# Full 128 x 128 tiles for every matmul of a pooling-attention and MLP-mixer kernel: padding in place of 64-row and 64-column operands

## The chip, the core and the metric

One core of a Trainium2 chip runs the whole kernel. The time is the device time of one launch in microseconds (us), from the first instruction to the last. The kernel before takes 377.35 us, the median of 4 runs (375.98 to 378.72).

## What is computed

Two networks one after the other, for 8 batch elements of 576 positions. First an attention of 8 heads of 64, whose keys and values are averaged over groups of 8 positions, so that there are 72 of each. Then a mixer: an MLP over the positions (256 wide) and an MLP over the channels (1536 wide), each added to its input.

```python
# q, k, v: (8, 8, 576, 64) float32
k_p = k.reshape(B, H, 72, 8, D).mean(axis=3)
v_p = v.reshape(B, H, 72, 8, D).mean(axis=3)
scores = 1/sqrt(D) * (q @ k_p.transpose(0, 1, 3, 2))
attn = softmax(scores)
x = (attn @ v_p) -> (B, 576, 512)
u = x + (relu(x^T @ w_tok1) @ w_tok2)^T       # w_tok1 576 x 256, w_tok2 256 x 576
out = u + relu(u @ w_ch1) @ w_ch2             # w_ch1 512 x 1536, w_ch2 1536 x 512
```

## The kernel before

All matmuls are bf16 with sums in float32. 576 positions are four chunks of 128 and a tail of 64; `csize = [128, 128, 128, 128, 64]`. TensorE (PE) multiplies a stationary operand `lhsT`, loaded into the array by a weight load (PEld), with a moving operand `rhs`; the profile gives the two as rows of `lhsT` * columns of `lhsT`, so 128*64 is an `lhsT` of 128 rows and 64 columns. Three stages stand for one batch element each. Stage A is the attention:

```python
# pool k (pool v, s_pool_v, is the same into its own bank, after all of k)
            for c in range(NC):
                cs = csize[c]
                nc.tensor.matmul(out=kp_ps, lhsT=p_full[0:cs, c, :], rhs=kb[0:cs, c].rearrange("p h d -> p (h d)"),
                                 start=(c == 0), stop=(c == NC - 1))
            nc.vector.tensor_copy(out=kp_sb, in_=kp_ps)
# transpose the pooled k, head by head: 64 columns each, to partitions 0..63 or 64..127
            for h in range(H):
                pr, hl = h // 2, h % 2
                nc.tensor.transpose(out=kpT_ps[hl * D:(hl + 1) * D, pr, 0:SP], in_=kp_sb[:, h, :],
                                    identity=ident[0:SP, 0:SP])
            nc.vector.tensor_copy(out=kpT_sb, in_=kpT_ps[:, :, 0:SP])
# transpose q
                qT_ps = ps_tr.tile([P, H // 2, P], BF16, name="pt")
                for pr in range(H // 2):
                    nc.tensor.transpose(out=qT_ps[:, pr, 0:cs],
                                        in_=qb[0:cs, c, 2 * pr:2 * pr + 2, :].rearrange("p h d -> p (h d)"),
                                        identity=ident[0:cs, 0:cs])
                nc.scalar.copy(out=qT_sb[:, :, c * P:c * P + cs], in_=qT_ps[:, :, 0:cs])
# scores of one head: 64 rows of lhsT
            def s_score():
                pr, hl = h // 2, h % 2
                sc_ps = ps_big.tile([SP, 512], FP32, name="pa")
                sc_ps2 = ps_small.tile([SP, S - 512], FP32, name="pb")
                nc.tensor.matmul(out=sc_ps, lhsT=kpT_sb[hl * D:(hl + 1) * D, pr, :],
                                 rhs=qT_sb[hl * D:(hl + 1) * D, pr, 0:512], start=True, stop=True)
                nc.tensor.matmul(out=sc_ps2, lhsT=kpT_sb[hl * D:(hl + 1) * D, pr, :],
                                 rhs=qT_sb[hl * D:(hl + 1) * D, pr, 512:S], start=True, stop=True)
                nc.scalar.activation(out=expT_sb[:, h, 0:512], in_=sc_ps, func=AF.Exp, scale=scale)
                nc.scalar.activation(out=expT_sb[:, h, 512:S], in_=sc_ps2, func=AF.Exp, scale=scale)
# attention times v, for one chunk and four heads; the 65th column is the sum of exp
                cs = csize[c]
                ao_ps = ps_small.tile([P, 4, D + 1], FP32, name="pb")
                for hh in range(4):
                    h = half * 4 + hh
                    nc.tensor.matmul(out=ao_ps[0:cs, hh, :], lhsT=expT_sb[:, h, c * P:c * P + cs],
                                     rhs=vp_sb[:, h, :], start=True, stop=True)
                den_r = out_pool.tile([P, 4], FP32, name="den")
                nc.vector.reciprocal(out=den_r[0:cs], in_=ao_ps[0:cs, :, D])
                bcast = den_r[0:cs, :, None].broadcast_to([cs, 4, D])
                nc.vector.tensor_tensor(out=x_sb[0:cs, c, half * 4 * D:(half + 1) * 4 * D].rearrange("p (h d) -> p h d", d=D),
                                        in0=ao_ps[0:cs, :, 0:D], in1=bcast, op=ALU.mult)
# ...
        steps += [mk_av(c, half) for c in range(NC) for half in range(2)]
```

Stage B is the MLP over the positions, stage C the one over the channels:

```python
# stage B
                at_ps = ps_big.tile([P, DM], FP32, name="pa")
                for c in range(NC):
                    cs = csize[c]
                    nc.tensor.matmul(out=at_ps, lhsT=w_tok1_sb[0:cs, c, m * P:(m + 1) * P], rhs=x_sb[0:cs, c, :],
                                     start=(c == 0), stop=(c == NC - 1))
# ...
                u_ps = ps_big.tile([P, DM], FP32, name="pa")
                for m in range(2):
                    nc.tensor.matmul(out=u_ps[0:cs, :], lhsT=w_tok2_sb[:, m, c * P:c * P + cs], rhs=AT_sb[:, m, :],
                                     start=(m == 0), stop=(m == 1))
                nc.vector.tensor_tensor(out=u_sb[0:cs, c, :], in0=u_ps[0:cs, :], in1=x_sb[0:cs, c, :], op=ALU.add)
                uT_ps = ps_tr.tile([P, 4, P], BF16, name="pt")
                for kk in range(4):
                    nc.tensor.transpose(out=uT_ps[:, kk, 0:cs], in_=u_sb[0:cs, c, kk * P:(kk + 1) * P],
                                        identity=ident[0:cs, 0:cs])
# ... copied to uT by ScalarE (c even) or VectorE (c odd)
# stage C
                g_ps = ps_big.tile([P, 512], FP32, name="pa")
                g_ps2 = ps_small.tile([P, S - 512], FP32, name="pb")
                for kk in range(4):
                    nc.tensor.matmul(out=g_ps, lhsT=w_ch1_sb[:, kk, m * P:(m + 1) * P], rhs=uT_sb[:, kk, 0:512],
                                     start=(kk == 0), stop=(kk == 3))
                for kk in range(4):
                    nc.tensor.matmul(out=g_ps2, lhsT=w_ch1_sb[:, kk, m * P:(m + 1) * P], rhs=uT_sb[:, kk, 512:S],
                                     start=(kk == 0), stop=(kk == 3))
# ... relu to GT on ScalarE (m even) or VectorE (m odd)
            def s_out():
                cs = csize[c]
                o_ps = ps_big.tile([P, DM], FP32, name="pa")
                for kk in range(12):
                    nc.tensor.matmul(out=o_ps[0:cs, :], lhsT=GT_sb[:, kk, c * P:c * P + cs], rhs=w_ch2_sb[:, kk, :],
                                     start=(kk == 0), stop=(kk == 11))
                o_sb = out_pool.tile([P, DM], FP32, name="o")
                nc.vector.tensor_tensor(out=o_sb[0:cs, :], in0=o_ps[0:cs, :], in1=u_sb[0:cs, c, :], op=ALU.add)
                nc.scalar.dma_start(out=out[b, c * P:c * P + cs, :], in_=o_sb[0:cs, :])
```

PSUM, in which matmuls put their sums, is handed out from three pools: `ps_big` (tiles "pa", 4 buffers), `ps_small` (tiles "pb", 2 buffers) and `ps_tr` (tiles "pt" of transposes, 2 buffers). The stages are a software pipeline: in turn `it` the kernel runs A of element `it`, B of element `it - 1` and C of element `it - 2`, their steps woven into one another. So there are 10 turns, of which turns 2 to 7 hold all three stages. The loads of `q`, `k` and `v` for the next element are DMAs that GpSimd issues at the start of a turn; the four weight matrices are loaded at the start of the kernel.

Of the kernel before, what the change touches and what calls it, by code (L numbers as in the profile page):

```python
# [8 lines left out]
FP32 = mybir.dt.float32  # L9
# [6 lines left out]
def kernel(  # L16
# [48 lines left out]
    w_tok2_sb = singles.tile([P, 2, S], BF16)  # L65
# [3 lines left out]
    with tc.tile_pool(name="wtmp", bufs=1) as wtmp:  # L69
# [9 lines left out]
        nc.vector.tensor_copy(out=w_tok2_sb, in_=wf2)  # L79
# [22 lines left out]

    def stage_A(qb, kb, vb, x_sb):
        kp_sb = att_pool.tile([SP, H, D], BF16, name="kp")
        vp_sb = att_pool.tile([SP, H, D + 1], BF16, name="vp")
        kpT_sb = att_pool.tile([P, H // 2, SP], BF16, name="kpT")
        qT_sb = att_pool.tile([P, H // 2, S], BF16, name="qT")
        expT_sb = att_pool.tile([SP, H, S], BF16, name="expT")
        steps = []

        def s_pool_k():
            kp_ps = ps_big.tile([SP, H, D], FP32, name="pa")
            for c in range(NC):
                cs = csize[c]
                nc.tensor.matmul(out=kp_ps, lhsT=p_full[0:cs, c, :], rhs=kb[0:cs, c].rearrange("p h d -> p (h d)"),  # L115
                                 start=(c == 0), stop=(c == NC - 1))
            nc.vector.tensor_copy(out=kp_sb, in_=kp_ps)
        def s_pool_v():
            vp_ps = ps_big.tile([SP, H, D], FP32, name="pa")
            for c in range(NC):  # L120
                cs = csize[c]
                nc.tensor.matmul(out=vp_ps, lhsT=p_full[0:cs, c, :], rhs=vb[0:cs, c].rearrange("p h d -> p (h d)"),  # L122
                                 start=(c == 0), stop=(c == NC - 1))
            nc.gpsimd.memset(vp_sb[:, :, D], 1.0)  # L124
            nc.vector.tensor_copy(out=vp_sb[:, :, 0:D], in_=vp_ps)
        def s_kpT():
            kpT_ps = ps_tr.tile([P, H // 2, P], BF16, name="pt")
            for h in range(H):
                pr, hl = h // 2, h % 2
                nc.tensor.transpose(out=kpT_ps[hl * D:(hl + 1) * D, pr, 0:SP], in_=kp_sb[:, h, :],  # L130
                                    identity=ident[0:SP, 0:SP])
            nc.vector.tensor_copy(out=kpT_sb, in_=kpT_ps[:, :, 0:SP])
        steps += [s_pool_k, s_pool_v, s_kpT]

        def mk_qT(c):
            def s_qT():
                cs = csize[c]
                qT_ps = ps_tr.tile([P, H // 2, P], BF16, name="pt")
                for pr in range(H // 2):
                    nc.tensor.transpose(out=qT_ps[:, pr, 0:cs],  # L140
                                        in_=qb[0:cs, c, 2 * pr:2 * pr + 2, :].rearrange("p h d -> p (h d)"),
                                        identity=ident[0:cs, 0:cs])
# [4 lines left out]
        def mk_score(h):  # L147
            def s_score():
# [3 lines left out]
                nc.tensor.matmul(out=sc_ps, lhsT=kpT_sb[hl * D:(hl + 1) * D, pr, :],  # L152
                                 rhs=qT_sb[hl * D:(hl + 1) * D, pr, 0:512], start=True, stop=True)
                nc.tensor.matmul(out=sc_ps2, lhsT=kpT_sb[hl * D:(hl + 1) * D, pr, :],  # L154
                                 rhs=qT_sb[hl * D:(hl + 1) * D, pr, 512:S], start=True, stop=True)
# [5 lines left out]
        def mk_av(c, half):  # L161
            def s_av():
                cs = csize[c]
                ao_ps = ps_small.tile([P, 4, D + 1], FP32, name="pb")
                for hh in range(4):
                    h = half * 4 + hh
                    nc.tensor.matmul(out=ao_ps[0:cs, hh, :], lhsT=expT_sb[:, h, c * P:c * P + cs],  # L167
                                     rhs=vp_sb[:, h, :], start=True, stop=True)
                den_r = out_pool.tile([P, 4], FP32, name="den")
                nc.vector.reciprocal(out=den_r[0:cs], in_=ao_ps[0:cs, :, D])  # L170
                bcast = den_r[0:cs, :, None].broadcast_to([cs, 4, D])
                nc.vector.tensor_tensor(out=x_sb[0:cs, c, half * 4 * D:(half + 1) * 4 * D].rearrange("p (h d) -> p h d", d=D),  # L172
                                        in0=ao_ps[0:cs, :, 0:D], in1=bcast, op=ALU.mult)
            return s_av
        steps += [mk_av(c, half) for c in range(NC) for half in range(2)]
        return steps

    def stage_B(x_sb, u_sb, uT_sb):
        AT_sb = moe_pool.tile([P, 2, DM], BF16, name="AT")
        steps = []  # L180
        def mk_AT(m):
            def s_AT():
                at_ps = ps_big.tile([P, DM], FP32, name="pa")
                for c in range(NC):
                    cs = csize[c]
                    nc.tensor.matmul(out=at_ps, lhsT=w_tok1_sb[0:cs, c, m * P:(m + 1) * P], rhs=x_sb[0:cs, c, :],  # L186
# [8 lines left out]
        def mk_u(c):  # L195
            def s_u():
                cs = csize[c]
                u_ps = ps_big.tile([P, DM], FP32, name="pa")
                for m in range(2):
                    nc.tensor.matmul(out=u_ps[0:cs, :], lhsT=w_tok2_sb[:, m, c * P:c * P + cs], rhs=AT_sb[:, m, :],  # L200
# [14 lines left out]
    def stage_C(b, u_sb, uT_sb):  # L215
        GT_sb = moe_pool.tile([P, 12, S], BF16, name="GT")
# [51 lines left out]
    for it in range(B + 2):  # L268
# [5 lines left out]
        if ba < B:  # L274
# [5 lines left out]
            x_sb = x_pool.tile([P, NC, DM], BF16, name="x")  # L280
            xbuf[ba] = x_sb
            A_steps = stage_A(qb, kb, vb, x_sb)
# [43 lines left out]
```

The softmax here doesn't subtract the row's maximum and nothing guards it: scores larger than these inputs give would overflow.

## Time and profile before

| what | value |
|---|---|
| time, median of 4 runs | 377.35 us |
| span of the profiled run | 377.0 us |
| TensorE matmul busy | 329.2 us, 87% of the span, 2280 recorded |
| TensorE weight load busy | 161.1 us, 43% |
| VectorE busy | 160.8 us, 43% |
| ScalarE busy | 117.7 us, 31% |
| GpSimd busy | 106.3 us, 28% |
| DMA | 31.44 MB, mean 83 GB/s |

Engines: PE is a TensorE matmul, PEld a TensorE weight load, which runs beside matmuls; DVE is VectorE, ACT ScalarE, POOL GpSimd. "L223" is line 223 of the kernel. The end of a matmul in the profile is modelled and matmuls overlap in the array, so the duration of one says little; the distance from one start to the next is what one costs in a stream. A few per cent of the matmul records are missing from the trace.

### The profile page before, as it was taken

Reading aid. Unit: us, or ns where it says so; the run is one execution under the profiler, and the core shown is the slowest. Engines: PE = TensorE matmul, PEld = TensorE weight load, DVE = VectorE, ACT = ScalarE, POOL = GpSimd, SP = SyncE. Lnnn points to the kernel's source line nnn. Section 1 sums busy time; section 2 is a strip of 40 time slices with the busy share of each in tenths; the row PEclk is TensorE's granted clock in tenths of the full one; section 3 lists DMA queues with packets and bytes.
Section 4 is the critical chain, followed back from the end, with each engine's and each line's share of the span. In section 5 each row is a group of like instructions: output and inputs, shape, how many; then the busy total and the mean of one; then the engine's idle time right before and its main releaser. Section 6 shows DMA issues by size and latency. Waiting matters only on the chain.

```text
span 377.0 us, 5649 instructions
## 1 busy us (share of the span) xinstructions
PE 329.2 (87%) x2280; PEld 161.1 (43%) x2320; DVE 160.8 (43%) x389; ACT 117.7 (31%) x299; POOL 106.3 (28%) x138
## 2 busy tenths in 40 slices
PE   0305459899999999999999999999999999999994
PEld 0003125355454544444545454445445454544542
DVE  1003026382655345634553365445552654443421
ACT  1005406527501660056104720364017501310300
POOL 9819369946103900193008400000000000000000
PEclk9999999999999999999999999999999999999999
DMA  9999999979823971299029902000210011002012
GB/s 137 235 291 123 314 166 117 147 51 104 54 76 66 129 46 57 70 124 66 30 84 106 98 13 99 16 2 0 86 42 2 1 71 57 0 28 92 7 57 70
DMA packets 120746, 31.44 MB, mean 83 GB/s; under 512 B 113232, under 2 KB 113808, under 8 KB 120720
## 3 DMA queue, kind: packets, MB, share of 16 engines
q0 software_dynamic: 112512, 14.16, 63.8%
q10 hardware_dynamic: 5248, 9.44, 7.2%
q1 hardware_dynamic: 2960, 7.47, 5.8%
q8 instruction: 18, 0.29, 0.3%
q14 instruction: 8, 0.07, 0.1%
HBM read 35.78 MB, written 9.44 MB: 120 GB/s over the span
## 4 chain that ended last, share of the span: by engine, by line
PE 82%; DMA 8%; POOL 5%; ACT 2%; issue 1%; DVE 1%; POOLq 0%
PE pa L242 27%; PE pa L223 23%; DMA kb<-in_k_dram 8%; PE pa L186 5%; PE pa L200 5%; PE pb L167 4%; PE pa L152 3%; PE pb L226 3%; PE pt L205 3%; PE pa L122 3%; PE pt L140 2%; PE pa L115 2%; POOL qb L99 2%; POOL vb L99 2%; POOL kb L99 1%
## 5 line engine op out<-in xcount | busy, mean ns | idle before, releaser
L242 PE MATMUL pa<-w_ch_sb,GT 128*128 128x512 bf16 (+1 forms) x472 | 111.9, 379 | 0.4
L223 PE MATMUL pa<-uT,w_ch_sb 128*128 128x512 bf16 x363 | 95.7, 380 | 2.0 <-issue 1.3
L242 PEld LDWEIGHTS <-GT 128*128 128x128 bf16 (+1 forms) x480 | 45.1, 100 | 45.3 <-issue 0.8
L245 DVE TENSOR_TENSOR o<-pa,u 128x512 f32<-128x512 f32 (+1 forms) x40 | 27.6, 690 | 58.2 <-PE pa L242 56.2
L232 DVE TENSOR_SCALAR GT<-pa 128x512 bf16<-128x512 f32 x48 | 33.1, 691 | 36.8 <-PE pa L223 36.6
L223 PEld LDWEIGHTS <-w_ch_sb 128*128 128x128 bf16 x384 | 31.7, 98 | 31.8 <-issue 7.7
L229 ACT ACTIVATE GT<-pa 128x512 bf16<-128x512 f32 x48 | 28.7, 597 | 52.6 <-PE pa L223 50.8
L208 ACT COPY uT<-pt 128x512 bf16<-128x512 bf16 (+1 forms) x24 | 12.3, 514 | 103.2 <-PE pt L205 103.2
L156 ACT ACTIVATE expT<-pa 72x512 bf16<-72x512 f32 x64 | 37.9, 599 | 18.6 <-PE pb L154 18.3
L115 PE MATMUL pa<-kb,p_full 128*72 128x512 bf16 (+1 forms) x40 | 14.4, 441 | 30.3 <-DMA kb<-in_k_dram 30.3
L99 POOL DMA_DIRECT2D vb<-in_v_dram x40 | 36.3, 915 | 13.8 <-DMA qb<-in_q_dram 11.9
L202 DVE TENSOR_TENSOR u<-pa,x 128x512 bf16<-128x512 f32 (+1 forms) x40 | 27.1, 677 | 30.4 <-PE pa L200 28.1
L143 ACT COPY qT<-pt 128x512 bf16<-128x512 bf16 (+1 forms) x40 | 21.1, 551 | 59.7 <-PE pt L140 59.1
L99 POOL DMA_DIRECT2D qb<-in_q_dram x40 | 35.3, 891 | 10.5 <-PE pt L140 5.8
L99 POOL DMA_DIRECT2D kb<-in_k_dram x40 | 35.1, 881 | 10.6 <-PE pt L205 9.4
L172 DVE TENSOR_TENSOR x<-pb,den 128x256 bf16<-128x256 f32 (+1 forms) x80 | 32.8, 417 | 1.3
L226 PEld LDWEIGHTS <-w_ch_sb 128*128 128x128 bf16 x384 | 23.4, 98 | 18.1 <-issue 0.2
L124 POOL MEMSET vp<- 72x8 bf16 x8 | 1.5, 186 | 94.8 <-issue 94.8
L167 PEld LDWEIGHTS <-expT 72*128 72x128 bf16 (+1 forms) x320 | 19.5, 106 | 17.9 <-issue 5.4
L226 PE MATMUL pb<-uT,w_ch_sb 128*128 128x64 bf16 x384 | 26.5, 193 | 0.1
L200 PE MATMUL pa<-AT,w_tok_sb 128*128 128x512 bf16 (+1 forms) x71 | 25.0, 408 | 1.2 <-ACT AT L189 0.8
L186 PE MATMUL pa<-x,w_tok_sb 128*128 128x512 bf16 (+1 forms) x78 | 24.3, 410 | 0.1
(44 smaller groups left out, 258.1 us busy)
## 6 DMA issues: line engine op xcount, KB each, us to landing
out_dram<-o ACTq DMA_DIRECT2D x32, 256.0 KB, 2.0
wf<-in_moe_w_ch_dram SPq DMA_DIRECT2D x2, 3072.0 KB, 13.8
qb<-in_q_dram POOLq DMA_DIRECT2D x32, 128.0 KB, 4.6
kb<-in_k_dram POOLq DMA_DIRECT2D x32, 128.0 KB, 4.7
vb<-in_v_dram POOLq DMA_DIRECT2D x32, 128.0 KB, 5.0
out_dram<-o ACTq DMA_DIRECT2D x8, 128.0 KB, 2.3
wf<-in_moe_w_tok_dram SPq DMA_DIRECT2D x1, 576.0 KB, 5.8
wf<-in_moe_w_tok_dram SPq DMA_DIRECT2D x1, 512.0 KB, 3.8
```

The costliest lines, as they stand in the source:

```text
L99: nc.gpsimd.dma_start(out=dst[0:cs, c], in_=src_[b, :, c * P:c * P + cs, :].rearrange("h p d -> p h d"))
L156: nc.scalar.activation(out=expT_sb[:, h, 0:512], in_=sc_ps, func=AF.Exp, scale=scale)
L167: nc.tensor.matmul(out=ao_ps[0:cs, hh, :], lhsT=expT_sb[:, h, c * P:c * P + cs], rhs=vp_sb[:, h, :], start=True, stop=True)
L172: nc.vector.tensor_tensor(out=x_sb[0:cs, c, half * 4 * D:(half + 1) * 4 * D].rearrange("p (h d) -> p h d", d=D), in0=ao_ps[0:cs, :, 0:D], ...
L186: nc.tensor.matmul(out=at_ps, lhsT=w_tok1_sb[0:cs, c, m * P:(m + 1) * P], rhs=x_sb[0:cs, c, :], start=(c == 0), stop=(c == NC - 1))
L200: nc.tensor.matmul(out=u_ps[0:cs, :], lhsT=w_tok2_sb[:, m, c * P:c * P + cs], rhs=AT_sb[:, m, :], start=(m == 0), stop=(m == 1))
L223: nc.tensor.matmul(out=g_ps, lhsT=w_ch1_sb[:, kk, m * P:(m + 1) * P], rhs=uT_sb[:, kk, 0:512], start=(kk == 0), stop=(kk == 3))
L226: nc.tensor.matmul(out=g_ps2, lhsT=w_ch1_sb[:, kk, m * P:(m + 1) * P], rhs=uT_sb[:, kk, 512:S], start=(kk == 0), stop=(kk == 3))
L229: nc.scalar.activation(out=GT_sb[:, m, 0:512], in_=g_ps, func=AF.Relu)
L232: nc.vector.tensor_scalar(out=GT_sb[:, m, 0:512], in0=g_ps, scalar1=0.0, scalar2=None, op0=ALU.max)
L242: nc.tensor.matmul(out=o_ps[0:cs, :], lhsT=GT_sb[:, kk, c * P:c * P + cs], rhs=w_ch2_sb[:, kk, :], start=(kk == 0), stop=(kk == 11))
L245: nc.vector.tensor_tensor(out=o_sb[0:cs, :], in0=o_ps[0:cs, :], in1=u_sb[0:cs, c, :], op=ALU.add)
```

## The change

Every matmul and every weight load gets more than 64 rows and more than 64 columns, by padding:

- The tail chunk of 64 positions is treated as 128. The tiles of `q`, `k`, `v`, `x`, `u` (rows) and of the exponentials, `GT` and `w_tok2` (columns) are made 640 positions long; what lies behind position 576 is set to zero once, at the start, and is never written again. So these tiles are no longer handed out by rotating pools: there are two of each, made once, and taken in turns.
- The scores of a head contract over 64 channels. The stationary operand becomes 128 rows, of which the 64 that belong to the other head of the pair are zero; the moving operand becomes both heads' q. The zeros are set once, and the copy of the transposed pooled k fills the other half.
- The pooled k is transposed in pairs of heads (4 transposes of 128 columns in place of 8 of 64), and copied out in 2 pieces in place of one.
- The pooling of k and that of v alternate chunk by chunk, in two banks, in place of all of k and then all of v.
- Attention times v handles both halves of the heads of a chunk in one step, alternating between the two "pb" buffers.

What is written to memory is the same 576 positions.

```diff
-    w_tok2_sb = singles.tile([P, 2, S], BF16)
+    w_tok2_sb = singles.tile([P, 2, NC * P], BF16)
 ...
+    kpT_z = [singles.tile([P, H, SP], BF16, name=f"kpTz{i}") for i in range(2)]
+    for t in kpT_z:
+        nc.vector.memset(t, 0.0)
+    SPAD = NC * P
+
+    def two(name, shape):
+        ts = [singles.tile(shape, BF16, name=f"{name}{i}") for i in range(2)]
+        for t in ts:
+            nc.vector.memset(t[TAIL:P, NC - 1], 0.0)
+        return ts
+    q_z, k_z, v_z = (two(n, [P, NC, H, D]) for n in ("qz", "kz", "vz"))
+    e_z = [singles.tile([SP, H, SPAD], BF16, name=f"ez{i}") for i in range(2)]
+    g_z = [singles.tile([P, 12, SPAD], BF16, name=f"gz{i}") for i in range(2)]
+    for t in e_z + g_z:
+        nc.vector.memset(t[:, :, S:SPAD], 0.0)
+    nc.vector.memset(w_tok2_sb[:, :, S:SPAD], 0.0)
+    x_z, u_z = (two(n, [P, NC, DM]) for n in ("xz", "uz"))
+
     def load_qkv(b):
-        qb = qkv_pool.tile([P, NC, H, D], BF16, name="qb")
-        kb = qkv_pool.tile([P, NC, H, D], BF16, name="kb")
-        vb = qkv_pool.tile([P, NC, H, D], BF16, name="vb")
+        qb, kb, vb = q_z[b % 2], k_z[b % 2], v_z[b % 2]
 ...
+    def stage_A(b, qb, kb, vb, x_sb):
 ...
-        kpT_sb = att_pool.tile([P, H // 2, SP], BF16, name="kpT")
+        kpT_sb = kpT_z[b % 2]
         qT_sb = att_pool.tile([P, H // 2, S], BF16, name="qT")
-        expT_sb = att_pool.tile([SP, H, S], BF16, name="expT")
+        expT_sb = e_z[b % 2]
 ...
         def s_pool_k():
             kp_ps = ps_big.tile([SP, H, D], FP32, name="pa")
+            vp_ps = ps_big.tile([SP, H, D], FP32, name="pa")
+            stage_A.vp_ps = vp_ps
             for c in range(NC):
                 cs = csize[c]
-                nc.tensor.matmul(out=kp_ps, lhsT=p_full[0:cs, c, :], rhs=kb[0:cs, c].rearrange("p h d -> p (h d)"),
+                nc.tensor.matmul(out=kp_ps, lhsT=p_full[:, c, :], rhs=kb[:, c].rearrange("p h d -> p (h d)"),
+                                 start=(c == 0), stop=(c == NC - 1))
+                nc.tensor.matmul(out=vp_ps, lhsT=p_full[:, c, :], rhs=vb[:, c].rearrange("p h d -> p (h d)"),
                                  start=(c == 0), stop=(c == NC - 1))
             nc.vector.tensor_copy(out=kp_sb, in_=kp_ps)
         def s_pool_v():
-            vp_ps = ps_big.tile([SP, H, D], FP32, name="pa")
-            for c in range(NC):
-                cs = csize[c]
-                nc.tensor.matmul(out=vp_ps, lhsT=p_full[0:cs, c, :], rhs=vb[0:cs, c].rearrange("p h d -> p (h d)"),
-                                 start=(c == 0), stop=(c == NC - 1))
+            vp_ps = stage_A.vp_ps
             nc.gpsimd.memset(vp_sb[:, :, D], 1.0)
             nc.vector.tensor_copy(out=vp_sb[:, :, 0:D], in_=vp_ps)
         def s_kpT():
             kpT_ps = ps_tr.tile([P, H // 2, P], BF16, name="pt")
-            for h in range(H):
-                pr, hl = h // 2, h % 2
-                nc.tensor.transpose(out=kpT_ps[hl * D:(hl + 1) * D, pr, 0:SP], in_=kp_sb[:, h, :],
+            for pr in range(H // 2):
+                nc.tensor.transpose(out=kpT_ps[:, pr, 0:SP],
+                                    in_=kp_sb[:, 2 * pr:2 * pr + 2, :].rearrange("p h d -> p (h d)"),
                                     identity=ident[0:SP, 0:SP])
-            nc.vector.tensor_copy(out=kpT_sb, in_=kpT_ps[:, :, 0:SP])
+            for hl in range(2):
+                nc.vector.tensor_copy(out=kpT_sb[hl * D:(hl + 1) * D, hl:H:2, :],
+                                      in_=kpT_ps[hl * D:(hl + 1) * D, :, 0:SP])
 ...
-                    nc.tensor.transpose(out=qT_ps[:, pr, 0:cs],
-                                        in_=qb[0:cs, c, 2 * pr:2 * pr + 2, :].rearrange("p h d -> p (h d)"),
-                                        identity=ident[0:cs, 0:cs])
+                    nc.tensor.transpose(out=qT_ps[:, pr, :],
+                                        in_=qb[:, c, 2 * pr:2 * pr + 2, :].rearrange("p h d -> p (h d)"),
+                                        identity=ident)
 ...
-                nc.tensor.matmul(out=sc_ps, lhsT=kpT_sb[hl * D:(hl + 1) * D, pr, :],
-                                 rhs=qT_sb[hl * D:(hl + 1) * D, pr, 0:512], start=True, stop=True)
-                nc.tensor.matmul(out=sc_ps2, lhsT=kpT_sb[hl * D:(hl + 1) * D, pr, :],
-                                 rhs=qT_sb[hl * D:(hl + 1) * D, pr, 512:S], start=True, stop=True)
+                nc.tensor.matmul(out=sc_ps, lhsT=kpT_sb[:, h, :],
+                                 rhs=qT_sb[:, pr, 0:512], start=True, stop=True)
+                nc.tensor.matmul(out=sc_ps2, lhsT=kpT_sb[:, h, :],
+                                 rhs=qT_sb[:, pr, 512:S], start=True, stop=True)
 ...
-        def mk_av(c, half):
+        def mk_av(c):
             def s_av():
                 cs = csize[c]
-                ao_ps = ps_small.tile([P, 4, D + 1], FP32, name="pb")
+                ao = [ps_small.tile([P, 4, D + 1], FP32, name="pb") for _ in range(2)]
                 for hh in range(4):
-                    h = half * 4 + hh
-                    nc.tensor.matmul(out=ao_ps[0:cs, hh, :], lhsT=expT_sb[:, h, c * P:c * P + cs],
-                                     rhs=vp_sb[:, h, :], start=True, stop=True)
-                den_r = out_pool.tile([P, 4], FP32, name="den")
-                nc.vector.reciprocal(out=den_r[0:cs], in_=ao_ps[0:cs, :, D])
-                bcast = den_r[0:cs, :, None].broadcast_to([cs, 4, D])
-                nc.vector.tensor_tensor(out=x_sb[0:cs, c, half * 4 * D:(half + 1) * 4 * D].rearrange("p (h d) -> p h d", d=D),
-                                        in0=ao_ps[0:cs, :, 0:D], in1=bcast, op=ALU.mult)
+                    for half in range(2):
+                        h = half * 4 + hh
+                        nc.tensor.matmul(out=ao[half][:, hh, :], lhsT=expT_sb[:, h, c * P:(c + 1) * P],
+                                         rhs=vp_sb[:, h, :], start=True, stop=True)
+                for half in range(2):
+                    den_r = out_pool.tile([P, 4], FP32, name="den")
+                    nc.vector.reciprocal(out=den_r[0:cs], in_=ao[half][0:cs, :, D])
+                    bcast = den_r[0:cs, :, None].broadcast_to([cs, 4, D])
+                    nc.vector.tensor_tensor(out=x_sb[0:cs, c, half * 4 * D:(half + 1) * 4 * D].rearrange("p (h d) -> p h d", d=D),
+                                            in0=ao[half][0:cs, :, 0:D], in1=bcast, op=ALU.mult)
             return s_av
-        steps += [mk_av(c, half) for c in range(NC) for half in range(2)]
+        steps += [mk_av(c) for c in range(NC)]
 ...
-                    nc.tensor.matmul(out=at_ps, lhsT=w_tok1_sb[0:cs, c, m * P:(m + 1) * P], rhs=x_sb[0:cs, c, :],
+                    nc.tensor.matmul(out=at_ps, lhsT=w_tok1_sb[:, c, m * P:(m + 1) * P], rhs=x_sb[:, c, :],
 ...
-                    nc.tensor.matmul(out=u_ps[0:cs, :], lhsT=w_tok2_sb[:, m, c * P:c * P + cs], rhs=AT_sb[:, m, :],
+                    nc.tensor.matmul(out=u_ps, lhsT=w_tok2_sb[:, m, c * P:(c + 1) * P], rhs=AT_sb[:, m, :],
 ...
-                    nc.tensor.transpose(out=uT_ps[:, kk, 0:cs], in_=u_sb[0:cs, c, kk * P:(kk + 1) * P],
-                                        identity=ident[0:cs, 0:cs])
+                    nc.tensor.transpose(out=uT_ps[:, kk, :], in_=u_sb[:, c, kk * P:(kk + 1) * P],
+                                        identity=ident)
 ...
-        GT_sb = moe_pool.tile([P, 12, S], BF16, name="GT")
+        GT_sb = g_z[b % 2]
 ...
-                    nc.tensor.matmul(out=o_ps[0:cs, :], lhsT=GT_sb[:, kk, c * P:c * P + cs], rhs=w_ch2_sb[:, kk, :],
+                    nc.tensor.matmul(out=o_ps, lhsT=GT_sb[:, kk, c * P:(c + 1) * P], rhs=w_ch2_sb[:, kk, :],
 ...
-            x_sb = x_pool.tile([P, NC, DM], BF16, name="x")
+            x_sb = x_z[ba % 2]
 ...
-            u_sb = moe_pool.tile([P, NC, DM], BF16, name="u")
+            u_sb = u_z[bb % 2]
```

More of the change, by code (lines that the diff above doesn't have):

```diff
@@ L78 @@
         nc.sync.dma_start(out=wf2, in_=moe_w_tok2.rearrange("(c p) n -> p c n", p=P))
-        nc.vector.tensor_copy(out=w_tok2_sb, in_=wf2)
+        nc.vector.tensor_copy(out=w_tok2_sb[:, :, 0:S], in_=wf2)
         wf3 = wtmp.tile([P, 4, DC], FP32, name="wf")
@@ L101, in load_qkv @@
         return (qb, kb, vb), [go]
-    def stage_A(qb, kb, vb, x_sb):
+    def stage_A(b, qb, kb, vb, x_sb):
         kp_sb = att_pool.tile([SP, H, D], BF16, name="kp")
         vp_sb = att_pool.tile([SP, H, D + 1], BF16, name="vp")
-        kpT_sb = att_pool.tile([P, H // 2, SP], BF16, name="kpT")
+        kpT_sb = kpT_z[b % 2]
         qT_sb = att_pool.tile([P, H // 2, S], BF16, name="qT")
-        expT_sb = att_pool.tile([SP, H, S], BF16, name="expT")
+        expT_sb = e_z[b % 2]
         steps = []
@@ L279 @@
                 pre += ld
-            x_sb = x_pool.tile([P, NC, DM], BF16, name="x")
+            x_sb = x_z[ba % 2]
             xbuf[ba] = x_sb
-            A_steps = stage_A(qb, kb, vb, x_sb)
+            A_steps = stage_A(ba, qb, kb, vb, x_sb)
         if 0 <= bb < B:
             x_prev = xbuf.pop(bb)
-            u_sb = moe_pool.tile([P, NC, DM], BF16, name="u")
+            u_sb = u_z[bb % 2]
             uT_sb = moe_pool.tile([P, 4, S], BF16, name="uT")
```

## The prediction

> **What bounds the kernel now.** I read the page's busy shares first, then the stretches of the run, then the chain, then the matmuls in order of time. The busy shares make TensorE (PE) the suspect. The answer by stretches (start:end, length, busy time of each engine, granted clock, DMA share, GB/s) says where:
>
> ```profile
> PE 329.2 (87%) x2280; PEld 161.1 (43%) x2320; DVE 160.8 (43%) x389; ACT 117.7 (31%) x299; POOL 106.3 (28%) x138
> ...
> PE 82%; DMA 8%; POOL 5%; ACT 2%; issue 1%; DVE 1%; POOLq 0%
> ```
>
> ```profile
> 0.00:53.00 53.00, 15.69 (x60) 5.93 (x61) 5.75 (x8) 11.33 (x23) 34.63 (x48) 1.00 1.74 216
> 53.00:78.35 25.35, 23.80 (x147) 11.27 (x148) 14.50 (x38) 12.14 (x25) 20.65 (x26) 1.00 2.31 124
> ...
> 118.00:157.60 39.60, 38.96 (x286) 19.45 (x291) 19.32 (x49) 13.90 (x37) 12.73 (x16) 1.00 0.79 75
> ...
> 316.00:346.90 30.90, 30.69 (x192) 14.56 (x197) 13.09 (x28) 6.31 (x16) 0.00 (x0) 1.00 0.11 39
> 346.90:377.00 30.10, 25.06 (x158) 12.03 (x160) 9.34 (x19) 4.64 (x13) 0.00 (x0) 0.99 0.14 44
> ```
>
> The first 53 us are loading: PE has 15.7 us of work and waits for data. From 53 to 78.35 us is turn 1, the second attention with the first position MLP. Then six full turns (2 to 7) of 39.60 us each follow, to 316 us, in which PE is busy for 38.96 us and no other engine for half the time. Turn 8 (30.9 us) and turn 9 (about 25 us and the last store) have no attention. So from 53 us on, what shortens PE's stream shortens the run.
>
> PE at 98% busy could look like PE at its limit, but the ends of matmuls are modelled. So I read starts. Columns: start, length, line, matmul, count. A matmul of 128x512 repeats every 216 ns (12 of L242 take 2.59 us in the chain), one of 64 columns every 29 ns, one of 128 every 56 ns, when they follow their like:
>
> ```profile
> 245.48 0.28 PE L226 MATMUL pb<-uT,w_ch_sb 128*128 128x64 bf16 x4
> 245.59 0.39 PE L140 MATMUL pt<-ident,qb 128*128 128x128 bf16 x4
> ...
> 249.52 0.28 PE L226 MATMUL pb<-uT,w_ch_sb 128*128 128x64 bf16 x4
> 249.73 0.40 PE L152 MATMUL pa<-qT,kpT 64*72 64x512 bf16 x1
> 249.97 0.19 PE L154 MATMUL pb<-qT,kpT 64*72 64x64 bf16 x1
> 250.10 1.04 PE L223 MATMUL pa<-uT,w_ch_sb 128*128 128x512 bf16 x4
> ```
>
> Four small L226 matmuls followed by a 128*128 transpose take 0.11 us (245.48 to 245.59). The same four followed by a score with 64 rows take 0.21 us (249.52 to 249.73), and leaving the score costs again: the 64-column L154, worth 0.03 us, holds PE for 0.13 us (249.97 to 250.10). I took the starts of all matmuls of a turn in pairs and set the usual distance of the first of each pair off. Pairs that go from a tile of over 64 rows and columns to one of 64 rows or 64 columns, or back, have 88 to 103 ns left over, mostly 93; pairs of the same kind nearly all have under 12. Operands of 72 rows or columns behave like 128. None of these gaps is named as a wait: the engine has nothing to wait for.
>
> **What the Trainium skill says.** TensorEngine Tiling (Array Packing), section Key Properties: changing the tiling mode, and not just the tile, drains TensorE. The trace agrees, and prices it at about 93 ns for each direction. TensorE: Matmul & The Clock Gate, section LDWEIGHTS (loading the stationary operand): a load's time follows its columns and not its rows. The trace agrees: 99 ns for 64*128 and 101 ns for 128*128 at L186, so padding rows is free there. Same page, Part 1: the array runs at half its clock until PE has been busy for a window of about 3.4 us. The trace bears this out below the granted clock, which shows 1.00 throughout: until about 76.5 us a 128x512 matmul repeats every 0.43 us, then every 0.216. Two rows show it; the second of the two matmuls ends 1.04 us after the first's start in the one, 0.59 us in the other:
>
> ```profile
> 74.12 1.04 PE L200 MATMUL pa<-AT,w_tok_sb 128*128 128x512 bf16 x2
> ...
> 84.32 0.59 PE L223 MATMUL pa<-uT,w_ch_sb 128*128 128x512 bf16 x2
> ```
>
> Perfetto Trace Analysis, Per-instruction lifecycle: the reported end of a matmul is an estimate, which is why I use starts.
>
> **The change, part by part.**
>
> Removed: the switches. In the order of a full turn I count them: pool k tail in and out, pool v tail in, to the 64-column transposes of pooled k, and out of them (5 in all); the two tails of L186 in, of which one goes out to a full tile and the other on to a score (3); q's tail in and out (2); the eight scores, some of them in pairs with only a full matmul between (15 with the last way out); the tail of attention times v and the tails of the output and of u, which follow one another with 64 columns (2). That makes 27. The pairs of starts show 25 of them in the turn from 236.8 us, 2.46 us in sum; two hide behind missing records. 27 x 93 ns = 2.5 us.
>
> Added on PE: eight transposes of q's and u's tails become 128 wide, 8 x (56 - 29) ns = 0.22 us. Removed: four of the eight transposes of pooled k, some 4 x 30 ns = 0.12 us. Padded rows and columns of the stationary operand add no streaming time, as a matmul's 216 ns depends on the moving columns alone (the output's 128*64 and 128*128 at L242 both repeat every 216 ns). So the array's work rises by 0.1 us.
>
> Waits that stay or move. Of a turn's 39.60 us some 0.75 us is left over in pairs without a switch. The largest, 0.48 us between two scores at 251.4 us, is a "pb" buffer that ScalarE has not emptied:
>
> ```profile
> 251.94 0.19 PE L154 MATMUL pb<-qT,kpT 64*72 64x64 bf16 x1 [0.32 <-ACT GT L230]
> ```
>
> In the changed order, which I took from the built program, the second score of such a pair stands one 512-column matmul later, and the relu it waits on moves to VectorE; so perhaps half of this wait goes. Against it, attention times v now takes both "pb" buffers at once, and VectorE needs 2 x (0.17 + 0.42) = 1.2 us to empty them. Between two such steps stand 12 output matmuls, 2.59 us, so this fits with the 0.69 us of the output's own addition. At the end of a turn it is tighter: VectorE has the output's addition, both halves and u's addition to do, 0.69 + 1.2 + 0.69 = 2.6 us, while PE has 0.26 + 0.43 + 9 x 0.216 = 2.6 us of work ahead of the transposes of u; up to 0.2 us may be lost. I let these cancel: a full turn saves 2.5 - 0.1 = 2.4 us, of which I keep 2.3 for what I overlook.
>
> Also added: about 20 small fills with zeros on VectorE in the first microseconds, when it has 5.75 us of work in 53, and one more copy of about 0.3 us per turn on VectorE. Both lie beside other work.
>
> The sum: six turns x 2.3 = 13.8 us, with 0.4 more for turn 2, whose weave shows 30 switches. Turn 8 has 8 switches, 0.78 us, less 0.1 for its wider transposes: 0.65. Turn 9 has 2 or 3: 0.2. Turn 1 has 28 at the slow clock, where one costs about 0.12 us, so 3.3 us with those of its last, fast part less; not all of it is on the path, as PE also waits there for ScalarE (0.76 us before 67.74) and for q's copies; and its transposes cost twice as much extra. I take 2. But its PE stream gets denser, and attention times v of element 0 no longer stands behind all of pool k, which waits for the last keys until 52.14 us. So the fast clock may come earlier than 76.5 us, and each 2 us of slow work made fast gives 1 us. I take another 2. Together 13.8 + 0.4 + 0.65 + 0.2 + 4 = 19 us, and 377.35 - 19 = 358.3; I say 358.5.
>
> **The rivals.**
>
> 1. A wait takes the place of the drain. The drains gave ScalarE and VectorE time to empty PSUM; in the stretch of the scores ScalarE has 8 x 0.58 us of exponentials (two in a row start at 251.77 and 252.35 us) and over 3 us of relus and copies in some 10 us. If it became the bound there, or if "pb" with its two buffers did, PE would stop at scores for 0.2 to 0.3 us in each turn's several places: half the gain goes, about 367 us. For it: one such wait exists already. Against it: ScalarE does 13.9 us in 39.6, catches up directly afterwards, and the switched score pairs stand further apart in the new order.
>
> 2. The gaps are no mode switches but waits for weight loads, which cannot be pulled ahead of a matmul. Then padding would not remove them, the transposes would add their 0.2 us and the time would be 375 to 379 us. Against it: 72-row operands with their own weight loads show no gap, and the gap is nearly the same for 512-column and 64-column neighbours, though a 512-column matmul would hide a load of 0.1 us.
>
> 3. The opening decides: it is loading until 53 us and stays so, but the slow clock may last as long as before, or end 8 us earlier. This spans 361 to 354 us.
>
> **Range and chances.** Rival 3 gives some 4 us to either side. A full turn's saving between 1.9 and 2.6 us gives 11.4 to 15.6, 2 us to either side. Range 352 to 365 us. Within 2% means above 369.8 us, which needs a loss of over half the switch gain: rival 1 in its strong form or rival 2. Faster by over 2%: 0.94, within 2%: 0.05, slower: 0.01.
>
> **What would show it.** Right: full turns of about 37.3 us; no extra distance between the starts around a score (0.03 us for the small score, as for L226); the matmuls in stretches of a turn busy no less than before; the loading until about 53 us unchanged. Wrong: distances of 0.12 us still there (rival 2), PE waits put down to ScalarE or VectorE at scores or at attention times v (rival 1), or 128x512 matmuls every 0.43 us beyond 80 us (the opening).

## The result, and the profile after

| | before | after |
|---|---|---|
| median | 377.72 us (375.54 to 379.01, 16 runs) | 356.25 us (354.45 to 358.44, 11 runs) |
| ratio | | 0.9443, 95% interval 0.9417 to 0.9468 |
| span of the profiled run | 377.0 us | 353.1 us |

The changed kernel is 5.6% faster; 358.5 us was predicted. In the page of the changed kernel, first the busy shares and then the shares of the chain:

```profile
PE 308.0 (87%) x2246; PEld 160.7 (46%) x2288; DVE 165.0 (47%) x414; ACT 116.9 (33%) x299; POOL 106.5 (30%) x138
...
PE 78%; DMA 8%; POOL 6%; ACT 5%; issue 1%; DVE 0%; ACTq 0%; POOLq 0%
```

TensorE is as busy a share of the span as before, 87%, and still the bound. Before, that number hid about 20 us of drains (215 switches in the program at 93 ns, an estimate), and now it doesn't show that they are gone; busy time is no measure of what TensorE gets done. The other engines do the same work as before within 5 us.

The stretches of the changed kernel, cut at the first pool k matmul of turn 2 (67.97 us), of turn 3 (106.71) and of turn 5 (181.44); columns as before:

```profile
49.20:57.40 8.20, 6.76 (x47) 4.13 (x48) 4.58 (x14) 2.25 (x4) 7.72 (x9) 0.51 2.74 149
57.40:67.97 10.57, 8.45 (x76) 4.71 (x75) 7.57 (x18) 9.64 (x22) 10.57 (x14) 1.00 2.03 126
67.97:106.71 38.74, 38.37 (x319) 20.72 (x323) 22.81 (x65) 13.86 (x38) 18.42 (x26) 1.00 1.25 103
...
181.44:218.81 37.37, 37.01 (x282) 19.53 (x286) 19.25 (x50) 13.75 (x37) 12.69 (x16) 1.00 0.85 80
```

A full turn is 37.37 us in place of 39.60. Turn 2 is 38.74 in place of 41.42 (76.47 to 117.89 us in the kernel before). And turn 2 starts at 67.97 us in place of 76.47. So the profiled runs differ by 8.5 us before turn 2, 2.7 in turn 2, 5 x 2.24 = 11.2 in turns 3 to 7, and the last 1.5 in turns 8 and 9 and in the end of the last store: 23.9 us in all. The medians differ by 21.5 us; the profiled run of the changed kernel took 354.82 us, near the lower end of its range, and that of the kernel before 378.72, near the upper end of its own.

A score between two relu groups, in order of time in the changed kernel (start, length, line, matmul, count):

```profile
200.98 0.28 PE L246 MATMUL pb<-uT,w_ch_sb 128*128 128x64 bf16 x4
201.09 0.39 PE L170 MATMUL pa<-qT,kpTz 128*72 128x512 bf16 x1
201.31 0.19 PE L172 MATMUL pb<-qT,kpTz 128*72 128x64 bf16 x1
201.34 1.03 PE L243 MATMUL pa<-uT,w_ch_sb 128*128 128x512 bf16 x4
```

From L246 to the score 0.11 us, where it was 0.21; from the small L172 to the next group 0.03 us, where it was 0.13. Both drains are gone. The only pairs of matmuls in a full turn that still have some 0.09 us left over are two transposes of u that wait for VectorE, as before. What is left over in a full turn is waits of 0.7 us in sum; the longest is again one for a "pb" buffer:

```profile
197.56 0.39 PE L170 MATMUL pa<-qT,kpTz 128*72 128x512 bf16 x1
...
198.05 0.19 PE L172 MATMUL pb<-qT,kpTz 128*72 128x64 bf16 x1
```

0.49 us from start to start where 0.22 is usual: 0.27 us of waiting.

One thing went the other way, and the prediction doesn't have it. In the kernel before, two neighbouring scores of a pair of heads, one on rows 0 to 63 of the array and one on rows 64 to 127, streamed at the same time:

```profile
255.12 0.41 PE L152 MATMUL pa<-qT,kpT 64*72 64x512 bf16 x2
255.37 0.19 PE L154 MATMUL pb<-qT,kpT 64*72 64x64 bf16 x1
255.49 0.39 PE L200 MATMUL pa<-AT,w_tok_sb 128*128 128x512 bf16 x1
255.88 0.19 PE L154 MATMUL pb<-qT,kpT 64*72 64x64 bf16 x1
```

The two L152 start 7 ns apart, and the next matmul starts 0.25 us after the first of them, as behind a single score. A full turn had two such pairs, so some 0.43 us of streaming was hidden; in the changed kernel every score streams by itself. The eight transposes of the pooled k also ran two at a time, 3 to 4 ns apart, so the four that padding removed save nothing. With the wider transposes (0.22 us) the array's work in a full turn thus grew by about 0.65 us, an estimate from these spacings, and not by the 0.1 us of the prediction.

### The profile page after: what moved, and what is told of

It reads as the page before. It is cut to its first block, busy times and chain, and to the rows that moved or that the text cites. A ratio compares the mean times of both kernels' runs of the same rounds, so it can differ in the third digit from the quotient of the medians.

```text
span 353.1 us, 5713 instructions
## 1 busy us (share of the span) xinstructions
PE 308.0 (87%) x2246; PEld 160.7 (46%) x2288; DVE 165.0 (47%) x414; ACT 116.9 (33%) x299; POOL 106.5 (30%) x138
## 4 chain that ended last, share of the span: by engine, by line
PE 78%; DMA 8%; POOL 6%; ACT 5%; issue 1%; DVE 0%; ACTq 0%; POOLq 0%
PE pa L262 29%; PE pa L243 22%; PE pa L220 5%; DMA vz<-in_v_dram 4%; PE pa L206 4%; DMA kz<-in_k_dram 4%; PE pb L246 3%; PE pt L225 3%; PE pb L186 3%; ACT ez L174 2%; PE pt L158 2%; PE pa L170 2%; PE pa L133 2%; PE pa L135 2%; POOL vz L115 2%; POOL kz L115 2%
## 5 line engine op out<-in xcount | busy, mean ns | idle before, releaser
L262 PE MATMUL pa<-w_ch_sb,gz 128*128 128x512 bf16 x464 | 110.1, 379 | 0.9
L262 PEld LDWEIGHTS <-gz 128*128 128x128 bf16 x480 | 44.5, 98 | 48.3 <-issue 1.0
L252 DVE TENSOR_SCALAR gz<-pa 128x512 bf16<-128x512 f32 x48 | 33.2, 691 | 47.5 <-PE pa L243 47.4
L265 DVE TENSOR_TENSOR o<-pa,uz 128x512 f32<-128x512 f32 (+1 forms) x40 | 27.6, 690 | 57.0 <-PE pa L262 57.0
L249 ACT ACTIVATE gz<-pa 128x512 bf16<-128x512 f32 x48 | 28.7, 599 | 57.4 <-PE pa L243 30.3
L174 ACT ACTIVATE ez<-pa 72x512 bf16<-72x512 f32 x64 | 37.9, 598 | 9.4 <-PE pb L172 8.4
L115 POOL DMA_DIRECT2D vz<-in_v_dram x40 | 38.7, 966 | 4.4 <-DMA qz<-in_q_dram 3.8
L115 POOL DMA_DIRECT2D kz<-in_k_dram x40 | 35.9, 898 | 9.7 <-DMA vz<-in_v_dram 7.6
L115 POOL DMA_DIRECT2D qz<-in_q_dram x40 | 35.7, 919 | 5.4 <-DMA kz<-in_k_dram 5.3
L246 PEld LDWEIGHTS <-w_ch_sb 128*128 128x128 bf16 x384 | 23.5, 98 | 19.7 <-issue 1.6
L192 DVE TENSOR_TENSOR xz<-pb,den 128x256 bf16<-128x256 f32 (+1 forms) x80 | 30.8, 416 | 0.3
L246 PE MATMUL pb<-uT,w_ch_sb 128*128 128x64 bf16 x384 | 26.5, 193 | 0.1
```

What stands on the lines that cost most here:

```text
L115: nc.gpsimd.dma_start(out=dst[0:cs, c], in_=src_[b, :, c * P:c * P + cs, :].rearrange("h p d -> p h d"))
L249: nc.scalar.activation(out=GT_sb[:, m, 0:512], in_=g_ps, func=AF.Relu)
L252: nc.vector.tensor_scalar(out=GT_sb[:, m, 0:512], in0=g_ps, scalar1=0.0, scalar2=None, op0=ALU.max)
L262: nc.tensor.matmul(out=o_ps, lhsT=GT_sb[:, kk, c * P:(c + 1) * P], rhs=w_ch2_sb[:, kk, :], start=(kk == 0), stop=(kk == 11))
```

## The experiments

**Order and padding apart.** The first kernel takes the kernel before and changes the order alone; the second takes the changed kernel and gives it the order of before.

```diff
 # e1: the kernel before, with
+            vp_ps = ps_big.tile([SP, H, D], FP32, name="pa")      # in s_pool_k
             for c in range(NC):
                 nc.tensor.matmul(out=kp_ps, lhsT=p_full[0:cs, c, :], rhs=kb[0:cs, c] ...)
+                nc.tensor.matmul(out=vp_ps, lhsT=p_full[0:cs, c, :], rhs=vb[0:cs, c] ...)
-        steps += [mk_av(c, half) for c in range(NC) for half in range(2)]
+        steps += [mk_av(c) for c in range(NC)]      # as in the change, but [0:cs] and c * P + cs
 # e2: the changed kernel, with s_pool_k, s_pool_v and mk_av(c, half) as before, on padded operands
```

> The kernel before with the new order alone (pool k and pool v in turns, both halves of attention times v in one step), all operands at their old sizes; 28 mode switches in a full turn in place of 27. Theory (the switches make the gain, and the denser stream without them brings the fast clock early): full turns 39.4 to 39.7 us, the fast clock not before 70 us, 374 to 378 us. Rival (the order brings the fast clock early, padding only the full turns): full turns the same, but the fast clock near 57 us and 366 to 371 us.

> The changed kernel with the order of before (all of pool k, then pool v; the two halves of attention times v as two steps), all padding kept; no mode switch at all. Theory (switches): full turns 37.3 to 37.7 us, the fast clock near 57 us, 355 to 359 us. Rival (order brings the clock): the same full turns, the fast clock near 70 us or later, 361 to 367 us.

Order alone: 371.36 us, ratio to before 0.984 (0.979 to 0.989). Its full turns are 39.63 us:

```profile
189.96:229.59 39.63, 39.63 (x292) 19.70 (x291) 19.00 (x49) 13.76 (x37) 12.71 (x16) 1.00 0.79 76
```

So the order brings nothing in the full turns, all in all. But in its opening two matmuls of 512 columns last 1.04 us together at 56.85 us and 0.59 us at 58.94: the clock is fast from about 58.7 us, and turn 2 starts at 69.0 us.

```profile
56.85 1.04 PE L188 MATMUL pa<-x,w_tok_sb 128*128 128x512 bf16 x2
...
58.94 0.59 PE L188 MATMUL pa<-x,w_tok_sb 128*128 128x512 bf16 x2
```

Padding alone: 359.73 us, ratio 0.951 (0.944 to 0.957), full turns 37.59 us, the clock fast from 57.9 us, turn 2 from 68.22 us. So e1 goes to the rival, but for 0.4 us, and e2 to the theory, but for 0.7: order alone brings the early clock, padding alone brings it too, and only padding shortens the full turns. Together they gain less than their sum (21.5 us against 7.4 + 19), as the opening can be gained only once. In a full turn the order is worth another 0.22 us beside the padding, most of it shorter waits for "pb".

**Part of the padding taken back.** Three kernels are the changed kernel with the scores, the tails' rows or the tails' columns at their old size:

```diff
 # e3
-  lhsT=kpT_sb[:, h, :],                      rhs=qT_sb[:, pr, 0:512]
+  lhsT=kpT_sb[hl * D:(hl + 1) * D, h, :],    rhs=qT_sb[hl * D:(hl + 1) * D, pr, 0:512]
 # e4: pooling, transposes of q and u, first position matmul
-  lhsT=w_tok1_sb[:, c, m * P:(m + 1) * P], rhs=x_sb[:, c, :]
+  lhsT=w_tok1_sb[0:cs, c, m * P:(m + 1) * P], rhs=x_sb[0:cs, c, :]
 # e5: attention times v, u, output
-  out=o_ps, lhsT=GT_sb[:, kk, c * P:(c + 1) * P]
+  out=o_ps[0:cs, :], lhsT=GT_sb[:, kk, c * P:c * P + cs]
```

> The changed kernel with the scores alone back on 64 rows, 118 switches in the program, 16 in a full turn. Theory (93 ns for each switch): full turns 37.37 + 16 x 0.094 = 38.9 us; 356.3 + 11.1 = 367 us, or up to 374 us if the switches in the opening also delay the fast clock. Rival (the gaps are weight loads that cannot be drawn ahead, whatever the size of tile): full turns at 37.4 us, 356 to 357 us.

> The changed kernel with the tail chunk back on 64 rows in the pooling, the transposes of q and u and the first position matmul; 66 switches in the program, 8 in a full turn, and eight transposes a turn 64 wide again (0.22 us less). Theory (93 ns for each switch): full turns 37.37 + 8 x 0.094 - 0.22 = 37.9 us; 356.3 + 66 x 0.094 - 8 x 0.22 = 360.7 us. Rival (a switch costs by the length of what is drained, so that the tails, mostly 512 columns, cost more than the scores): full turns over 38.3 us.

> The changed kernel with the tail back on 64 columns of the stationary operand in attention times v, in u and in the output; 25 switches in the program, only 2 in a full turn, as the three follow one another in the order. Theory (a switch costs, not the 64 columns themselves): full turns 37.37 + 2 x 0.096 = 37.55 us, 357 to 359 us. Rival (a 64-column operand costs by itself, for its 22 matmuls in a turn): full turns over 37.8 us.

| kernel | switches in a full turn | full turn | turn 2 starts | time | ratio to before |
|---|---|---|---|---|---|
| changed | 0 | 37.37 us | 67.97 us | 356.25 us | 0.944 (0.942 to 0.947) |
| e5, tail columns 64 | 2 | 37.61 | 69.97 | 359.61 | 0.954 (0.949 to 0.959) |
| e4, tail rows 64 | 8 | 38.01 | 69.91 | 363.3 | 0.960 (0.955 to 0.966) |
| e3, scores 64 rows | 16 | 38.51 | 68.87 | 364.1 | 0.967 (0.959 to 0.974) |
| before | 27 | 39.60 | 76.47 | 377.72 | 1 |

In e3 the drain is back, and only where the scores are:

```profile
207.33 0.28 PE L246 MATMUL pb<-uT,w_ch_sb 128*128 128x64 bf16 x4
207.54 0.40 PE L170 MATMUL pa<-qT,kpTz 64*72 64x512 bf16 x1
207.79 0.19 PE L172 MATMUL pb<-qT,kpTz 64*72 64x64 bf16 x1
207.91 0.61 PE L220 MATMUL pa<-AT,w_tok_sb 128*128 128x512 bf16 x2
```

0.21 us into the score and 0.12 us out of it, as in the kernel before, on the same weights and with the same sums. By pairs of starts the 16 switches of a turn cost 1.53 us, 96 ns each; those of e4 cost 98 each and the two of e5 93. So the price is the same for tails and scores, whether rows or columns are 64, and e5 shows that 64 columns cost nothing by themselves: 12 output matmuls of 128*64 in a row take 2.6 us, as those of 128*128 do.

But the turn of e3 is only 1.14 us longer, not the 1.53 us of its drains. Three waits of the changed kernel ahead of matmuls that write "pb", one of 0.27 us and two of 0.06, 0.39 us together, are not there: while TensorE drained, ScalarE and VectorE emptied buffers. A drain that covers a wait is worth less than it lasts. That is rival 1 in a small form. Two smaller terms about cancel: one pair of scores streams at the same time again (200.74 and 200.75 us, 0.22 us saved), and the small matmul follows a score of 64 rows some 27 ns later than one of 128 (0.18 us in the turn). The shorter turn is why the total of e3, expected at 367 us, came to 364.1; e4 and e5 came out 2.6 and 0.6 us above theirs; their turn 2 starts 2 us later than the changed kernel's.

**TensorE kept busy while it waits for keys.** In both kernels TensorE idles for most of the time from about 42 to 49 us. Extra matmuls, whose results nobody reads, fill that wait:

```diff
+    WARM = {1: {3: 30, 4: 8}}                 # element 1: 30 ahead of its chunk 3, 8 ahead of chunk 4
             for c in range(NC):               # in s_pool_k
+                if c in WARM.get(b, {}):
+                    scratch = ps_big.tile([P, 512], FP32, name="pa")
+                    for _ in range(WARM[b][c]):
+                        nc.tensor.matmul(out=scratch, lhsT=ident, rhs=kb[:, c - 1] ..., start=True, stop=True)
 # e11: the same with 64 of the 512 columns
```

> The kernel before with 38 extra matmuls of 512 columns (their results unused) while TensorE waits for the last keys of element 1; the built order then also puts attention times v of element 0 into that wait. Theory (the late fast clock alone accounts for what the opening gained beyond the switches): the clock is fast from about 46 us and stays so, turn 2 begins near 65 us in place of 76.5, full turns stay at 39.6 us, 365 to 369 us. Rival (the opening was slow by its waits for ScalarE and VectorE, and the clock matters little): turn 2 begins after 70 us, 371 us or more.

> The changed kernel with the same 38 extra matmuls. Theory: no slow stretch after 40 us (it was 47.0 to 57.3 us), turn 2 begins near 64 us in place of 68, full turns stay at 37.37 us, 351 to 354.5 us; 14 to 15 us under the kernel before with the same extra matmuls, which is what the switches are worth at the fast clock. Rival (the slow stretch is covered by loading and waits): 355 to 357 us.

> The kernel before with the same 38 extra matmuls at 64 columns, an eighth of the work, so that TensorE still idles in the wait; part of attention times v of element 0 moves into the wait as well. Theory (the work in the wait brings the clock, not that there are more instructions or another order): the clock slow beyond 60 us, turn 2 begins after 72 us, 373 to 377 us. Rival (any change of order is enough, as in the order-only kernel): the fast clock by 60 us, turn 2 before 70 us, 369 to 372 us.

The kernel before, kept busy: 369.67 us, ratio 0.981 (0.977 to 0.984). Its clock is fast from 46.0 us, its full turns are 39.61 us, and turn 2 starts at 68.11 us: 8.4 us earlier than before, 3 us later than expected; the pooling of the last keys, which stands behind the extra matmuls, starts at 54.98 us in place of 52.14.

The changed kernel, kept busy: 351.72 us, ratio 0.931 (0.926 to 0.936), the fastest of all kernels here. No slow stretch after 41 us, turn 2 starts at 64.67 us, full turns 37.37 us:

```profile
41.00:64.67 23.67, 22.20 (x173) 11.81 (x176) 12.87 (x33) 13.96 (x33) 15.01 (x18) 1.00 1.96 201
64.67:103.44 38.77, 38.40 (x315) 20.57 (x319) 23.02 (x65) 13.84 (x38) 22.60 (x30) 1.00 1.51 118
```

The two differ by 18 us, more than the 14 to 15 expected, for which I had left out the 32 switches of turn 1. Most of this difference is with the fast clock, which the one has from 41.0 us and the other from 46.0. The 215 switches of the whole program at 93 ns make 20 us; the added work of the array takes about 5 us of it (an estimate: 0.65 us for each of eight elements), and the rest, some 3 us in favour of the changed kernel, is not told apart here.

With the small filler: 373.17 us, ratio 0.988 (0.984 to 0.991). The result fell between theory and rival. The clock was slow from 47.3 to 60.9 us, as the 64-column matmuls left TensorE idle, but it then came 13 to 15 us earlier than in the kernel before, and turn 2 started at 70.53 us, 4.4 to 5.9 us earlier than in the two profiles of the kernel before. So the larger part of what the full filler gained in the opening came without dense work, from the changed order or from the 64-column matmuls themselves; the two are not separated.

**The same two kernels once more**, without an edit, to see how far the opening varies:

> The kernel before, unchanged, for a second profile. Theory (the late fast clock belongs to this kernel's opening): the clock fast between 70 and 78 us again, turn 2 begins at 75 to 77 us. Rival (76 us was a chance of one run): the fast clock anywhere from 57 us on.

> The changed kernel, unchanged, for a second profile. Theory: a slow stretch that ends by 62 us, turn 2 begins at 67 to 70 us, full turns of 37.37 us. Rival (chance): the slow stretch ends beyond 65 us and turn 2 begins beyond 71 us.

The changed kernel repeats itself: 354.49 us, slow from 45.4 to 59.1 us, turn 2 from 67.64 us, full turns 37.37 us. The kernel before doesn't (376.99 us):

```profile
52.36:60.40 8.04, 8.01 (x57) 4.52 (x56) 4.51 (x15) 1.75 (x3) 8.04 (x11) 1.00 3.45 146
60.40:67.30 6.90, 5.09 (x39) 2.00 (x37) 4.75 (x11) 6.35 (x11) 6.29 (x8) 1.00 2.28 119
67.30:74.10 6.80, 6.80 (x33) 2.70 (x33) 2.65 (x6) 3.40 (x10) 6.80 (x10) 0.50 2.35 150
```

Its clock turned fast at 60.4 us, was lost again at 67.3, and came back at 74.1; turn 2 started at 74.92 us. So my expectation of a single late change was wrong. In the fast stretch TensorE waited for the other engines (5.09 us of work in 6.90, the longest wait 0.78 us for AT from ScalarE), and it was slow again right after. What the two profiles of the kernel before share is that the fast clock comes for good only at 74 to 76 us.

**More buffers for the wait that is left.**

```diff
-ps_big bufs=4, ps_small bufs=2
+ps_big bufs=3, ps_small bufs=3
```

> The changed kernel with 3 buffers for pb and 3 for pa in place of 2 and 4. In the changed kernel a score waits about 0.27 us in each full turn for a pb buffer (197.56 to 198.05 us). If that is a buffer wait and three pa suffice: full turns 37.0 to 37.1 us, 354 to 355.5 us. If three pa are too few, new waits at 512-column groups: full turns over 37.5 us.

359.62 us, ratio 0.954 (0.950 to 0.958); full turns 37.36 us, the same as without, and between the two ranges expected. The wait for "pb" is gone, and others have come, at groups of 512 columns:

```profile
198.58 0.60 PE L220 MATMUL pa<-AT,w_tok_sb 128*128 128x512 bf16 x2
199.12 1.02 PE L243 MATMUL pa<-uT,w_ch_sb 128*128 128x512 bf16 x4
...
206.69 0.60 PE L220 MATMUL pa<-AT,w_tok_sb 128*128 128x512 bf16 x2
207.26 0.38 PE L170 MATMUL pa<-qT,kpTz 128*72 128x512 bf16 x1
```

Two matmuls of 512 columns should take 0.43 us; they hold TensorE for 0.54 and 0.57. Four such waits of 0.10 to 0.16 us make up for the one of 0.27. Its opening is slower too: turn 2 starts at 70.51 us and takes 40.42.

## Why the prediction was right, by its own steps

- The switches: right. 27 in a full turn, all gone, at 93 to 98 ns; e3, e4 and e5 bring the drain back where the operand is small and nowhere else. Rival 2 (weight loads, whatever the size) falls: the changed kernel has as many loads a turn as matmuls, all of 72 or 128 columns, and no such gap. What the 93 ns are made of stays open: at a switch the new load is not drawn ahead either (255.48 us for the L200 at 255.49 above), while in a stream it starts up to a whole matmul earlier, so an uncovered load may be part of them. And only the half on rows of what the prediction says of loads holds in this trace: 64 columns at L242 took 110 ns, 128 columns 98.
- A full turn: 2.3 us predicted, 2.24 measured, and partly by luck. The switches gave their 2.5 us, but the array's work grew by about 0.65 us and not by 0.1, since the scores and transposes that had streamed together no longer do. In return the time in neither switches nor the array's work fell from about 1.05 us to 0.68 (differences of the sums), which the prediction had kept nearly level. Turn 2: 2.7 predicted, 2.7 measured. Turns 8 and 9: 0.85 predicted; from the start of turn 8 to the last matmul the profiles give 56.30 and 55.46 us, 0.84.
- The waits: wrong in its largest line. The 0.48 us between two scores at 251.4 us was no wait of that length: the program has a matmul of u (L200) there, whose weight load stands in the trace at 251.54 us and whose matmul record is missing. That matmul and the switches on both its sides account for 0.40 us, and 0.08 us of waiting for "pb" is left, as at 255.88 above. In the changed kernel the wait for "pb" is 0.27 us. So it grew where half of it was to go: waits that the drains had covered came out, as e3 shows.
- The opening: right that the fast clock comes earlier, the size off. I took 2 us for switches and 2 for an earlier clock. By the pairs of profiles it is 8.5 us, or 7.3 in the second pair (74.92 to 67.64 us). The mis-sized term is the clock, as far as these runs tell: I let it come 4 us earlier, and it came for good 15 to 19 us earlier, at 57.3 and 59.1 us in place of 76.1 and 74.1. Half of 17 us is 8.5, of which waits for ScalarE and VectorE, seen in the stretch 57.40:67.97 (8.45 us of work in 10.57), took a part. The switches were undersized too, by a count of 28 in turn 1 where the program has 32.
- Also missed: that the new order would be enough for this by itself (e1). I had named it beside the density as one cause; the two were told apart only by the runs, and each suffices.

The sum, with 7.3 to 8.5 us for the opening in place of 4, is 354 to 355 us, which is where the two profiled runs stand (354.82 and 354.49 us); the median of the 11 runs is 356.25.

Left open: what the clock asks for. The prediction took the trace to bear out that one busy window of about 3.4 us brings the fast clock; it doesn't. In the kernel before TensorE has 3.41 us of work, by the profile's durations, in the 3.41 us from 52.24 us, and again from 62.48 us, and stays slow until 76.1; the changed kernel turned fast after a stretch with 2.85 us (53.87:57.28). I did not find a measure that sorts all the runs. So it is shown that changes to the opening move the clock, and not why.

## What to carry to other kernels

When TensorE is the bound, compare the starts of neighbouring matmuls, not busy time: a change between operands of over 64 rows and columns and smaller ones cost about 95 ns each way here, more than three small matmuls, and zeros up to the full tile removed it. The price of the zeros is small but not nothing: two small matmuls on different rows of the array can stream at the same time when they stand next to each other, and padded ones can't (0.43 us a turn here, against 2.5 us of switches). Count changes in the order that the program has on the engine, not small operands: 22 small matmuls in a row cost two. And where TensorE waits for its first data, work without use in that wait can pay (356.25 to 351.72 us here).

## What the runs showed of the hardware

- The clock. A matmul of 512 columns repeats every 0.43 or every 0.216 us where nothing holds it up. The granted-clock row shows 1.00 up to its first recorded change, although the starts say half, as in the first stretch of e9 above: 1.00, but two L122 matmuls take 1.05 us from 53.54 us; in the third stretch, at the same spacing, it shows 0.50. So the first slow stretch of a run must be read from the starts.
- The changes come on a grid. By the clock's records in the trace, from change to change it was 6.8 and 10.2 us in the changed kernel, 6.8 and 13.7 in its second profile, 6.8 and 6.8 in e9, 3.4 and 13.7 in e4: multiples of 3.4 us. The Trainium skill, TensorE: Matmul & The Clock Gate, Part 1, gives a free-running window of about 3.4 us; these runs agree.
- Over the runs of the changed kernel the time goes with the granted clock: spans of 352.7 us at a mean of 0.989 and 356.6 us at 0.970. In the kernel before it is the other way round. Of the 21 runs timed beside the experiments, 8 have a mean of 0.999 or 1.0 and take 378.2 to 379.5 us, and 12 have 0.989 to 0.991 and take 375.9 to 378.0. The two profiles show why: in the first (0.999) the slow stretch lies ahead of the first recorded change and is not in the mean, in the second (0.990) a later one is recorded. By this sign the 8.5 us of the first pair belong to the rarer and slower opening, the 7.3 us to the commoner.
